# Regrouping the local row loads of a sparse-attention and spectral-mixing kernel, with three edits of its tail

## Chip, cores, metric

One NeuronCore of a Trainium2 chip. The metric is device time in microseconds (us); lower is better. Engines have the profile's names: PE multiplies matrices, ACT is the scalar engine, DVE the vector engine, POOL is GpSimd, SP only issues transfers. "Clock" is the share of PE's full clock that was granted, "PSUM" the memory into which PE writes its results. A trace's span is some 1.8 us shorter than the time of the same run, so spans are compared with spans and times with times.

## The reference, cut to what matters

```python
def _attn_ref(q, k, v):                      # (8, 8, 576, 64), float32
    scores = q @ k.T / sqrt(D)
    # heads 0-3: causal, within 32 rows ("local"); heads 4-7: causal, same position mod 32 ("strided")
    attn = softmax(where(mask, scores, -1e9)); return attn @ v

def _moe_ref(x, w_r, w_i, w_ch):             # x: (8, 576, 512), w: (64, 512, 512)
    X = rfft(x, axis=1)[:, :64]              # 64 modes
    Y = X @ (w_r + 1j * w_i)                 # one 512x512 complex weight per mode
    u = x + irfft(Y, n=576)
    return u + maximum(u @ w_ch, 0)
```

The two weight arrays are 134 MB of float32, 163 MB are read in all. Each of the 64 modes needs weights of its own, 2 MB of float32, and the kernel takes each mode in two halves: 128 half-modes. One request for a pair brings the weights of two half-modes. Where the text and the timelines count modes ("mode 1", "mode 7", "the last mode"), they count half-modes from 0.

## The kernel before

All large loads are issued by GpSimd (POOL) on one queue, in program order, and are converted to fp16 on the way. The attention rows pass through one `ring`: strided rows of batch b take slots 3(b mod 4) to 3(b mod 4)+2, local rows of batch b take slots 2(b mod 6) and 2(b mod 6)+1.

```python
    ring = pat.tile([128, 12, 2048], F16, name="ring")
    ...
    def load_loc(*bs):                       # one batch's local rows per transfer, 288 KB
        for b in bs:
            if b >= B:
                return
            for vi in (2, 0, 1):             # v, q, k
                nc.gpsimd.dma_start(
                    loc_in(b, vi),
                    SRC[vi][b, 0:4].rearrange("h (cb i) d -> (h cb) (i d)", i=18),
                )
```

The strided stage is one iteration per batch. Its last iteration already turns local batch 0 (`loc_front(0)`). `w_fetch(1)` asks for one pair of half-modes (two transfers of 512 KB, from the two weight arrays); one pair is asked for before the loop. Eight pairs fit before any buffer has to be freed; three of the eight (pairs 1, 2 and 7) lie in buffers that are later needed for other things and are not refilled. So the first refill waits for mode 1, the second for mode 7.

```python
    for b in range(B):                       # strided stage
        if b in (1, 3):
            load_str(b + 3, 2)
        load_loc(*[(), (), (), (), (0,), (1, 2), (3,), (4, 5)][b])
        w_fetch([2, 1, 1, 1, 1, 1, 0, 0][b])
        front = str_front(b + 1) if b + 1 < B else loc_front(0)
        ...
    for b in range(B):                       # local stage, with the first 64 half-modes between
        load_loc(b + 6)
        front = loc_front(b + 1)
        ...
            mode(0, sum(NMODES[:b]) + mi)    # after an odd one: w_fetch() into the freed buffer
```

The tail: the last spectra are copied out of PSUM, then 36 units of 128 rows each get two short matmul groups (`v`, `u`), a Relu on ACT, an addition on DVE and a store. `again(n)` repeats a 512-column matmul n times, to keep PE's clock up while it waits for the last weights.

```python
    def spec_out(g, b, tp, zp):
        src, dst = ds(32 * (b % 4), 32), ds(32 * g, 32)
        n = 256 if (g, b) == (3, 0) else 512
        act_copy(zzs[b][dst, 0:n], zp[src, 0:n])              # ACT
        if n < 512:
            nc.vector.tensor_copy(out=zzs[b][dst, n:], in_=zp[src, n:])
        nc.vector.tensor_copy(out=yys[b][dst], in_=tp[src, 0:512])
    ...
            again(0 if m < NM - 6 else 4 if m < NM - 2 else 2)
```

The softmax here doesn't subtract the row's maximum and nothing guards it: scores larger than these inputs give would overflow.

## Time and profile before

| | before |
|---|---|
| time, median of the first 3 runs | 436.13 us (435.8 to 436.99) |
| span of the trace | 433.8 us |
| last weight landed / last mode began | 393.66 / 393.83 us |
| from the start of the last mode to the end | 40.0 us |
| time of the load queue's packets, share of the span | 94.3% |

The landing of the last weight is read from its issue (384.06) and the time to landing of that one transfer (9.6). A line of the profile reads: start and length, engine, source line, operation, written tile <- read tiles; in square brackets how long the engine had been idle before it, and what ended the wait. `wt` is a weight tile, `ring` the attention rows, `y` the modes' accumulators. The chain of waits of the kernel before carries the main reading, that the loads are the bound:

```profile
DMA 69%; PE 18%; DVE 6%; ACT 3%; issue 2%; POOL 1%; DVEq 0%; POOLq 0%
```

### The profile page before, as it was taken

The numbers are of one execution on the slowest core, as the hardware profiler recorded it, in microseconds if no ns is written. First come the engines' busy times: TensorE is split into PE (matmuls) and PEld (weight loads), VectorE is DVE, ScalarE is ACT, GpSimd is POOL, SyncE is SP. The second block draws the span as 40 slices with busy tenths as digits, with TensorE's granted clock in tenths as the row PEclk, the third lists the DMA queues.
The fourth block names the chain that finished last, engine by engine and source line by source line (L and its number), as shares of the span: only waits on it lengthen the run. The fifth ranks groups of instructions, "written<-read, shape, count | busy, mean of one in ns | idle before, by whom it ended". The sixth has DMA issues, their size and how long they took to land.

```text
span 433.8 us, 12099 instructions
## 1 busy us (share of the span) xinstructions
PE 338.7 (78%) x5307; PEld 244.0 (56%) x5307; DVE 215.1 (50%) x466; ACT 188.1 (43%) x353; POOL 128.9 (30%) x208
## 2 busy tenths in 40 slices
PE   1986888779886887889794566698669698977994
PEld 1865776657764665667663344465446465643441
DVE  2888678744523243342511033455346366503895
ACT  1686678635543435445340401133115122602892
POOL 6522332323232222222222222222222221200983
PEclk9999899869967659676855559868798899988999
DMA  8999999999999999999999999999999999991687
GB/s 178 212 213 213 215 212 212 212 210 213 215 212 214 213 214 213 213 214 214 213 213 213 213 213 215 213 213 215 213 213 213 214 213 213 214 179 29 260 331 275
DMA packets 28996, 92.18 MB, mean 212 GB/s; under 512 B 4048, under 2 KB 5072, under 8 KB 28944
## 3 DMA queue, kind: packets, MB, share of 16 engines
q0 software_dynamic: 24704, 81.28, 94.3%
q1 hardware_dynamic: 3440, 9.46, 5.8%
q10 hardware_dynamic: 800, 0.67, 0.6%
q8 instruction: 42, 0.69, 0.6%
q14 instruction: 10, 0.08, 0.0%
HBM read 163.22 MB, written 9.44 MB: 398 GB/s over the span
## 4 chain that ended last, share of the span: by engine, by line
DMA 69%; PE 18%; DVE 6%; ACT 3%; issue 2%; POOL 1%; DVEq 0%; POOLq 0%
DMA wt<-in_moe_w_i_dram 51%; DMA wt<-in_moe_w_r_dram 8%; DMA ring<-in_q_dram 5%; DMA w_ch<-in_moe_w_ch_dram 5%; DVE xb L250 2%; DVE kz L292 2%; PE y L547 2%; PE v L688 2%; PE u L688 2%; PE v L894 2%; PE sc L514 1%; ACT X L260 1%; DVE rec L249 1%; PE tp L395 1%; PE sc L353 1%
## 5 line engine op out<-in xcount | busy, mean ns | idle before, releaser
L547 PE MATMUL y<-X,wt 128*128 128x16 f16 (+1 forms) x2048 | 82.8, 192 | 59.5 <-DMA wt<-in_moe_w_i_dram 58.1
L547 PEld LDWEIGHTS <-wt 128*128 128x128 f16 (+1 forms) x2048 | 73.1, 103 | 75.4 <-issue 68.3
L196 POOL DMA_DIRECT2D wt<-in_moe_w_r_dram x62 | 36.4, 587 | 139.2 <-PE y L547 66.0
L196 POOL DMA_DIRECT2D wt<-in_moe_w_i_dram x60 | 35.2, 587 | 73.0 <-DMA wt<-in_moe_w_i_dram 60.2
L654 ACT ACTIVATE v<-sc 128x512 f16<-128x512 f32 x32 | 19.1, 596 | 68.4 <-PE sc L645 68.3
L471 ACT ACTIVATE PL<-sc 128x480 f16<-128x480 f32 (+1 forms) x48 | 27.7, 579 | 47.6 <-PE sc L457 46.9
L645 PE MATMUL sc<-w_cp,xT 128*128 128x512 f16 (+1 forms) x160 | 47.4, 424 | 0.0
L655 DVE COPY xo<-tp 128x512 f16<-128x512 f16 x32 | 22.1, 692 | 36.7 <-PE tp L653 36.4
L250 DVE TENSOR_TENSOR xb<-av,rec 90x256 f16<-90x256 f32 (+2 forms) x80 | 36.0, 450 | 2.8
L249 DVE RECIPROCAL rec<-av 90x4 f32<-90x4 f32 (+2 forms) x80 | 14.7, 183 | 45.3 <-PE av L486 33.9
L402 DVE COPY qT<-tp 128x576 f16<-128x576 f16 x16 | 12.0, 758 | 40.1 <-PE tp L395 37.2
L260 ACT ACTIVATE v<-tp 128x640 f16<-128x640 f16 (+1 forms) x24 | 19.4, 807 | 24.0 <-PE tp L429 21.1
L395 PE MATMUL tp<-cI_s,ring 64*64 64x64 f16 x864 | 26.4, 211 | 1.6 <-issue 0.8
L360 ACT ACTIVATE PL<-sc 90x360 f16<-90x360 f32 (+1 forms) x48 | 22.7, 490 | 6.2 <-PE sc L353 5.3
L926 DVE TENSOR_TENSOR osb<-u,rl 128x512 f32<-128x512 f32 x36 | 23.6, 689 | 3.3 <-ACT rl L907 1.7
L395 PEld LDWEIGHTS <-ring 64*64 64x64 f16 x864 | 20.7, 123 | 6.8 <-issue 3.6
L441 PE MATMUL sc<-cMl_s,cI_s 128*128 128x480 f16 (+1 forms) x48 | 23.0, 478 | 1.6 <-ACT X L260 1.6
L909 POOL TENSOR_TENSOR rl<-rl,xo 128x512 f32<-128x512 f32 x16 | 18.3, 1155 | 18.9 <-ACT rl L907 18.6
L457 PE MATMUL sc<-qT,kz 128*128 128x160 f16 (+1 forms) x160 | 23.4, 275 | 0.5 <-issue 0.5
L457 PEld LDWEIGHTS <-kz 128*128 128x128 f16 x160 | 16.8, 119 | 10.8 <-issue 8.1
L907 ACT ACTIVATE rl<-v 128x512 f32<-128x512 f32 x36 | 20.4, 597 | 4.9 <-PE v L688 4.2
L285 PE MATMUL tp<-cI_s,ring 72*128 72x72 f16 x256 | 15.1, 206 | 9.5 <-DMA ring<-in_v_dram 8.0
(103 smaller groups left out, 655.5 us busy)
## 6 DMA issues: line engine op xcount, KB each, us to landing
wt<-in_moe_w_r_dram POOLq DMA_DIRECT2D x62, 512.0 KB, 18.9
wt<-in_moe_w_i_dram POOLq DMA_DIRECT2D x60, 512.0 KB, 19.4
out_dram<-osb SPq DMA_DIRECT2D x14, 512.0 KB, 2.7
ring<-in_v_dram POOLq DMA_DIRECT2D x8, 288.0 KB, 13.4
ring<-in_q_dram POOLq DMA_DIRECT2D x8, 288.0 KB, 13.6
ring<-in_k_dram POOLq DMA_DIRECT2D x8, 288.0 KB, 13.0
ring<-in_v_dram POOLq DMA_DIRECT2D x3, 512.0 KB, 15.1
ring<-in_q_dram POOLq DMA_DIRECT2D x3, 512.0 KB, 14.8
```

The costliest lines, as they stand in the source:

```text
L196: nc.gpsimd.dma_start(dst, rows)
L250: nc.vector.tensor_tensor(out=dst, in0=val.rearrange("p h (q c) -> p h c q", c=4), in1=rec[0:n, 0:pieces] .to_broadcast((n, pieces, 64)) . ...
L260: nc.scalar.activation(out=out, in_=in_, func=ACTF.Copy)
L360: nc.scalar.activation(out=PS[0:n, ds(POFF[t], 4 * n)], in_=scp[0:n, 0 : 4 * n], func=ACTF.Exp, scale=SCALE,)
L395: nc.tensor.transpose(tp[ds(64 * hp, 64), ds(64 * i, 64)], qn[ds(64 * hp, 64), ds(64 * (9 * g + i), 64)], idn[ds(64 * hp, 64), ds(64 * hp, ...
L441: nc.tensor.matmul(scp[:, 0 : n * times].rearrange("p (h x) -> p h x", h=times), idn, mask_rows("cMl", n, times), start=True, stop=False,)
L457: nc.tensor.matmul(scp[:, ds(col, n)], kzs[par][:, hp, ds(s0, 128)], qTs[par][:, ds(s0, n)], start=False, stop=(i == len(todo) - 1),)
L471: nc.scalar.activation(out=dst, in_=src, func=ACTF.Exp, scale=SCALE)
L547: nc.tensor.matmul(yv[:, mi, e, :], wt[pr, XC[c], ds(128 * e, 128)], Xh[half][pr, c, :, :, m], start=(c == 0), stop=(c == 3),)
L645: nc.tensor.matmul(vp[pr, :], xT[:, ch, cols], w_chs["cp"][:, ch, :], start=(ch == 0), stop=(ch == 3),)
L655: nc.vector.tensor_copy(out=xo[pr].rearrange("p (h q c) -> p h q c", h=2, c=4), in_=tp[pr, 0:512].rearrange("p (h c q) -> p h q c", h=2, c=4),
L926: nc.vector.tensor_tensor(out=osb[:, t % 2, :], in0=up, in1=rls[b, t][:, t % 2, :], op=AluOp.add)
```

## The change

The intent: fewer, larger transfers (two batches' local rows in one), so that less is paid per transfer; one copy off ACT where ACT holds the tail's start; a finer last store, so that its first half leaves earlier; more repeated passes, so that PE's clock is up when the last weights land.

```diff
-    def load_loc(*bs):
-        for b in bs: ...
+    def load_loc(b):
+        for vi in (2, 0, 1):
+            two = ring[:, ds(2 * (b % 6), 4), :].rearrange("p (b n) x -> p b (n x)", b=2)
+            nc.gpsimd.dma_start(
+                two[:, :, ds(1152 * vi, 1152)],
+                SRC[vi][b : b + 2, 0:4].rearrange(
+                    "b h (cb i) d -> (h cb) b (i d)", i=18
+                ),
+            )
@@ spec_out
-        n = 256 if (g, b) == (3, 0) else 512
-        act_copy(zzs[b][dst, 0:n], zp[src, 0:n])
+        n = {(3, 0): 256, (3, 1): 0}.get((g, b), 512)
+        if n:
+            act_copy(zzs[b][dst, 0:n], zp[src, 0:n])
@@ strided stage
-        load_loc(*[(), (), (), (), (0,), (1, 2), (3,), (4, 5)][b])
-        w_fetch([2, 1, 1, 1, 1, 1, 0, 0][b])
+        w_fetch([2, 1, 1, 1, 2, 0, 0, 0][b])
+        if b > 4:
+            load_loc(2 * (b - 5))
@@ local stage
-        load_loc(b + 6)
+        if b == 1:
+            load_loc(6)
@@ last rows (cut)
+        halves = [ds(0, 256), ds(256, 256)] if i == LAST else [slice(None)]
+        for cols in halves: ...              # addition by halves; then one store per half,
+                                             # the first from ACT, the second from SP
@@ repeated passes
-            again(0 if m < NM - 6 else 4 if m < NM - 2 else 2)
+            again({NM - 1: 2, NM - 2: 3, NM - 3: 10}.get(m, 7 if m > NM - 6 else 0))
```

More of the change, by code (lines that the diff above doesn't have):

```diff
@@ L231, in load_str @@
                 nc.gpsimd.dma_start(two[64:72], src[64:72])
-    def load_loc(*bs):
-        for b in bs:
-            if b >= B:
-                return
-            for vi in (2, 0, 1):
-                nc.gpsimd.dma_start(
-                    loc_in(b, vi),
-                    SRC[vi][b, 0:4].rearrange("h (cb i) d -> (h cb) (i d)", i=18),
-                )
+    def load_loc(b):
[7 more added lines that the diff above has]
+            )
     def v_cols(i):
@@ L925, in u_rows @@
         osb = osbs[b, t]
-        nc.vector.tensor_tensor(
-            out=osb[:, t % 2, :], in0=up, in1=rls[b, t][:, t % 2, :], op=AluOp.add
-        )
+        halves = [ds(0, 256), ds(256, 256)] if i == LAST else [slice(None)]
+        for cols in halves:
+            nc.vector.tensor_tensor(
+                out=osb[:, t % 2, cols],
+                in0=up[:, cols],
+                in1=rls[b, t][:, t % 2, cols],
+                op=AluOp.add,
+            )
         if t == 4:
@@ L934, in u_rows @@
         elif i < 2 or i >= LAST - 1:
-            (nc.scalar if i == LAST else nc.sync).dma_start(
-                out[b, ds(128 * (t - t % 2), 256), :].rearrange(
-                    "(p i) e -> p i e", i=2
-                )[:, t % 2, :],
-                osb[:, t % 2, :],
-            )
+            for j, cols in enumerate(halves):
+                (nc.scalar if i == LAST and j == 0 else nc.sync).dma_start(
+                    out[b, ds(128 * (t - t % 2), 256), cols].rearrange(
+                        "(p i) e -> p i e", i=2
+                    )[:, t % 2, :],
+                    osb[:, t % 2, cols],
+                )
         elif t % 2:
```

## The prediction

> **What bounds the kernel now.** I read the page first (engine shares, slices, transfers), then the chain of waits, then Pool's timeline, then PE's timeline around each stage change.
>
> ```profile
> PEclk9999899869967659676855559868798899988999
> GB/s 178 212 213 213 215 212 212 212 210 213 215 212 214 213 214 213 213 214 214 213 213 213 213 213 215 213 213 215 213 213 213 214 213 213 214 179 29 260 331 275
> L547 PE MATMUL y<-X,wt 128*128 128x16 f16 (+1 forms) x2048 | 82.8, 192 | 59.5 <-DMA wt<-in_moe_w_i_dram 58.1
> ```
>
> The rate is flat at 213 GB/s from the second slice to the 35th: the load queue never runs dry until about 390 us. PE waits 58.1 us in total for weights. The chain of waits agrees: 51% of it is the transfer of the second weight array. So there are two parts: a **load stream** of fixed bytes (last weight used at 393.83 us) and a **tail** of 40 us, which the load stream no longer touches. A change pays only if it shortens the stream, stops it from pausing, or shortens the tail.
>
> Pool's timeline shows how the stream is fed.
>
> ```profile
> 58.64 0.57 POOL L238 DMA_DIRECT2D ring<-in_v_dram  x1 [2.21 <-PE tp L285]
> 59.21 0.56 POOL L238 DMA_DIRECT2D ring<-in_q_dram  x1
> ...
> 70.93 0.54 POOL L238 DMA_DIRECT2D ring<-in_v_dram  x1 [1.15 <-DMA ring<-in_v_dram]
> 72.07 0.54 POOL L238 DMA_DIRECT2D ring<-in_q_dram  x1 [0.60 <-DMA ring<-in_q_dram]
> 73.43 0.54 POOL L238 DMA_DIRECT2D ring<-in_k_dram  x1 [0.82 <-DMA ring<-in_k_dram]
> 75.88 0.60 POOL L196 DMA_DIRECT2D wt<-in_moe_w_r_dram  x1 [1.92 <-DMA wt<-in_moe_w_r_dram]
> ```
>
> The issue at 70.93 is the eighth after the one at 58.64, and it waits for that one to land. So eight transfers are outstanding, and these waits date the landings: batch 0's local v, q, k land at 70.9, 72.1 and 73.4. A 288 KB local transfer takes 1.40 us of stream, a 512 KB weight transfer 2.43. PE needs batch 0's q at 76.65:
>
> ```profile
> 76.65 0.76 PE L395 MATMUL tp<-cI_s,ring 64*64 64x64 f16 x36
> ...
> 79.03 0.47 PE L395 MATMUL tp<-cI_s,ring 64*64 64x64 f16 x18 [0.62 <-DVE qT L402]
> ...
> 95.05 0.62 PE L547 MATMUL y<-X,wt 128*128 128x16 f16 x16
> ...
> 102.99 0.67 PE L547 MATMUL y<-X,wt 128*128 128x16 f16 x16
> ```
>
> No wait for a transfer stands there: batch 0 is about 4 us early. The last two lines are modes 1 and 7, whose ends (95.67, 103.66) free the first two weight buffers for refilling.
>
> The tail, in windows of 3.4 us of PE, then by instruction:
>
> ```profile
> 391.50:394.90 3.40, 2.15 (x37) 0.97 0.14 28
> 394.90:398.30 3.40, 3.40 (x13) 0.53 0.02 5
> ```
>
> ```profile
> 394.85 1.89 PE L886 MATMUL y<-w_ch,YT 128*128 128x512 f16 x4
> ...
> 396.96 1.39 PE L951 MATMUL v<-v,cI_s 128*128 128x512 f16 x3
> ...
> 398.81 1.09 ACT L907 ACTIVATE rl<-v 128x512 f32<-128x512 f32 x2 [1.67 <-PE v L688]
> ...
> 399.93 0.59 ACT L260 ACTIVATE zz<-y 32x512 f16<-32x512 f32 x1
> ```
>
> Busy 2.15 of 3.4 us was followed by a window at clock 0.53 (columns: window, length, busy, clock, DMA share, GB/s). The first tail matmuls run at half rate.
>
> **What the Trainium skill says.**
> - "DMA: Bandwidth & Descriptors", section "Anatomy of one DMA — SWDGE (gpsimd) path": a transfer costs about 2.0 us fixed plus its bytes. Between queued transfers the trace shows none of it: 2.43 us for 512 KB is the stream's rate. It would be paid only when the queue is empty.
> - Same page, "Rules for kernel authors": coalesce small transfers into large ones. In a queue that is never empty, this case gives no sign of a gain.
> - "TensorE: Matmul & The Clock Gate", section on the HAM clock gate: the clock is halved after an idle window of about 3.4 us and restored after a busy one. The trace agrees on the length and the halving (clock 1.00 then 0.53); it shows also that a window 63% busy (2.15/3.4) did not keep the clock.
>
> **The change part by part.**
>
> (1) *Local rows in pairs.* 24 transfers of 288 KB become 12 of 576 KB; bytes and rows are the same. Per row 2304 bytes are still written. All that goes is 12 completions; I allow 0.3 us of stream at most (an estimate: two neighbouring local transfers already follow at 1.40 us, 211 GB/s, against 213 for weights; closing that gap over 33 us of local stream is 0.3 us).
>
> (2) *The new order.* A pair cannot be loaded before the fifth iteration, because it overwrites batch 5's strided v. So the order "batch 0, weights, 1, 2, weights, 3, 4, 5" becomes "weights, weights, 0+1, 2+3, 4+5". The transfer before batch 0's v lands at about 69.2 (Pool's issue of the last k then). Now four weight transfers come first, 4 x 2.43 = 9.7, to 79.0; then v 81.8, q 84.6, k 87.4 at 2.8 each. PE wants q at 76.65 and k at 79.03: it stalls about 8.4 us in the last strided iteration. PE is not the bound there, but it frees buffers. Shifted by 8.4, mode 1 ends at 104.1 and mode 7 at 112.1. The last loads that need no freed buffer (batches 4+5) land at 104.2 by the sum, 105.5 by the trace of the same bytes before. The next weights are issued at 104.2 and, with the skill's 2 us on an empty queue, start at 106.2; their pair takes 4.9, to 111.1; the pair after it waits for mode 7, is issued at 112.3 and starts at 114.3. Pauses: about 1.5 + 3 = 4.5 us. Before, batch 6's rows (4.2 us) filled that hole; now batches 6+7 are issued after the third of these. DVE, cleared during the stall, could win back half a microsecond: I take **+4.0 us**. The stream never makes up a pause, so all of it goes to the end.
>
> (3) *More repeated passes* (20 to 29, at 0.215 us warm). They fill the waits at 390.9 to 392.6 and 393.1 to 393.8, so PE is busy without a gap from mode 59 on. If the clock holds, the four matmuls of 1.89 us take 1.03 (they do so later in the tail), the three passes 0.65 instead of 1.39, mode 63 0.2 less. PE reaches the first spectra matmul 1.5 us earlier (398.40 to 396.9). DVE's second half copy then ends at about 396.5, not in the way. **-1.5 us.**
>
> (4) *Batch 1's copy to DVE.* On ACT 0.59 us goes between the second and third 597 ns activations, and PE waited for the third (0.24 idle, plus slow issue). DVE gains a 32x512 copy of about 0.68 (256 columns took 0.42, 512 of the same kind 0.69) before its first addition at 399.52, where it had 1.14 us idle. **-0.5 us.**
>
> (5) *Last rows in halves.*
>
> ```profile
> 426.91 1.89 DVE L926 TENSOR_TENSOR osb<-u,rl 128x512 f32<-128x512 f32 x3 [0.16 <-PE u L688]
> ...
> 428.23 0.62 SPq L935 DMA_DIRECT2D out_dram<-osb  x1
> 428.83 0.34 ACTq L935 DMA_DIRECT2D out_dram<-osb  x1
> ```
>
> The first half can leave 0.3 us earlier, the second at the same time or 0.1 later, since SP is free at 428.85. The writes queue on shared engines anyway, with 1 KB rows in place of 2 KB. **-0.2 us.**
>
> Sum: -0.3 + 4.0 - 1.5 - 0.5 - 0.2 = +1.5, on 436.1: **437.6 us**.
>
> **The rivals.**
> (A) *The pause is hidden.* If Pool finds buffers sooner, or PE's lag shrinks, the stream never stops: 436.1 - 2.5 = 433.6. For it: PE idles 58 us for weights, so it can catch up; a tuned order was presumably tried. Against: the first refills depend on modes 1 and 7, and PE was busy 7.94 of 8 us between 96 and 104.
> (B) *The pause is longer.* The stall cools PE's clock and the local stage starts at half rate, say 2 to 3 us later: 440.
> (C) *Passes too many.* With a cold clock ten passes last 4.3 us and overrun the wait after mode 61 by about 1 to 2 us; most of the 1.5 gain is lost: 439.
> (D) *Coalescing pays per transfer.* If each removed transfer saved 0.2 us of stream, 12 would save 2.4: 435.5. The flat rate speaks against it.
>
> **Range and chances.** All the terms are under 1.2% together. A and D pull down, B and C up: 433.6 to 441.0. A move of 2% is 8.7 us, which no rival reaches: within 2% 0.96, slower 0.03 (B and C together with a longer pause), faster 0.01.
>
> **What would show it.** Right: PE waits 7 to 9 us for local q near 77; batches 0+1 land at 84 to 88; a slice near 104 to 115 shows a dip of the rate; the last weight lands about 4 us later than 393.7; the window after it has clock 1.00; from the last mode to the end 38 us or less instead of 40. Wrong: no wait for q, no dip, or a half-rate window at the start of the tail. The largest risk is step 2: if the stream does not pause, the result is near 433.6.

## The result

The changed kernel took 440.82 us (median of 4 runs, 439.7 to 442.84) against 435.97 of the kernel before (4 runs, 434.8 to 436.99). Ratios in this document are the mean time of one kernel's fast runs over that of the other's of the same rounds, so they are not quite the ratio of the medians: here **1.0117**, 95% interval 1.0072 to 1.0162. It is slower by about 5 us, within the 2% that counts as "same", inside the stated range, in the stated direction, but three times the +1.5 us that was forecast.

The rate by slices, and the group of matmuls that turn local rows, from the page of the changed kernel:

```profile
GB/s 176 212 214 212 214 213 213 211 213 115 174 212 214 213 214 213 213 215 213 213 212 214 215 213 213 213 214 214 213 214 213 214 213 214 213 213 52 264 326 274
L395 PE MATMUL tp<-cI_s,ring 64*64 64x64 f16 x864 | 25.6, 210 | 8.9 <-DMA ring<-in_q_dram 8.3
```

The flat line of before now has a hole: slices 10 and 11 (98.5 to 120.4 us) ran at 115 and 174 instead of 213. That is (98 + 39) x 10.95 us / 213 = 7.0 us of stream lost. And PE waits 8.3 us for q, where it had no such wait. Pool's timeline of the changed kernel shows the order of events:

```profile
64.39 0.73 POOL L236 DMA_DIRECT2D ring<-in_v_dram  x1 [2.21 <-PE av L374]
65.12 0.72 POOL L236 DMA_DIRECT2D ring<-in_q_dram  x1
66.55 0.72 POOL L236 DMA_DIRECT2D ring<-in_k_dram  x1 [0.71 <-DMA wt<-in_moe_w_r_dram]
...
82.01 0.71 POOL L236 DMA_DIRECT2D ring<-in_k_dram  x1 [2.04 <-DMA ring<-in_v_dram]
105.49 0.60 POOL L196 DMA_DIRECT2D wt<-in_moe_w_r_dram  x1 [22.76 <-PE y L547]
106.08 0.60 POOL L196 DMA_DIRECT2D wt<-in_moe_w_i_dram  x1
112.63 0.59 POOL L196 DMA_DIRECT2D wt<-in_moe_w_r_dram  x1 [5.95 <-PE av L486]
```

After the last rows of the third pair, at 82.01, Pool has nothing that it may load: it is idle for 22.76 us until mode 1 frees the first weight buffer, and again for 5.95 us. That third pair landed 22.6 us after its issue, at 104.6; the next load was asked for at 105.49. PE's timeline of the changed kernel shows why mode 1 was so late:

```profile
84.54 1.17 PE L395 MATMUL tp<-cI_s,ring 64*64 64x64 f16 x36 [8.30 <-DMA ring<-in_q_dram]
...
87.33 1.17 PE L395 MATMUL tp<-cI_s,ring 64*64 64x64 f16 x36 [0.56 <-DMA ring<-in_k_dram]
...
104.53 0.66 PE L547 MATMUL y<-X,wt 128*128 128x16 f16 x16
```

The first line stood at 76.65 before, the last (mode 1) at 95.05: the stall moved mode 1 by 9.5 us. In windows of 2 us of the changed kernel (busy time of PE, weight load, DVE, ACT and Pool, then clock, DMA share and GB/s) the hole is this:

```profile
100.00:102.00 2.00, 1.16 (x14) 0.66 (x15) 0.00 (x0) 0.87 (x4) 0.00 (x0) 0.50 1.06 203
102.00:104.00 2.00, 2.00 (x37) 1.51 (x34) 0.76 (x1) 0.51 (x2) 0.00 (x0) 0.50 0.32 60
104.00:106.00 2.00, 2.00 (x55) 1.77 (x54) 0.37 (x1) 1.12 (x2) 0.51 (x1) 0.83 0.01 1
106.00:108.00 2.00, 2.00 (x67) 1.68 (x65) 1.95 (x5) 0.13 (x1) 0.68 (x2) 1.00 0.69 80
...
112.00:114.00 2.00, 1.99 (x61) 1.87 (x58) 1.43 (x4) 1.30 (x2) 1.18 (x2) 1.00 0.41 70
114.00:116.00 2.00, 1.89 (x33) 1.28 (x31) 0.49 (x1) 0.78 (x2) 1.24 (x3) 1.00 0.98 154
```

Two dips, one around each late request. From 102 on PE is busy throughout, so in this stretch the stream waits for PE, not PE for the stream. The issues of the two late requests, each looked up alone, give their time from issue to landing:

```profile
wt<-in_moe_w_r_dram POOLq DMA_DIRECT2D x1, 512.0 KB, 5.9
wt<-in_moe_w_r_dram POOLq DMA_DIRECT2D x1, 512.0 KB, 5.2
```

The first of them came to an empty queue; the second was issued 1.2 us before the pair ahead of it had landed (112.63 and 113.8). The packets in the trace show how the 5.9 us were spent. The load queue's first packet started at 106.79, 1.3 us after the request; from there to the landing it took 4.6 us, where transfers in the full stream follow one another at 2.43. The data started slowly: in steps of half a microsecond from 106.5 on, the rate was 147, 16, 156 and 156 GB/s before it came to 246. Why is open.

After 116 us the rate is flat again and the loss is carried to the end: the last weight landed at 399.95, 6.3 us later than before (393.66). The tail, from the start of the last mode, took 37.8 us instead of 40.0. The sum, 6.3 - 2.2 = 4.1, is the difference of the two spans (437.9 - 433.8). These are one trace each; the medians of the times differ by 4.9.

### The profile page after: what moved, and what is told of

The parts are those of the page before. It is cut to its first block, busy times and chain, and to the rows that moved or that the text cites. A ratio compares the mean times of both kernels' runs of the same rounds, so it can differ in the third digit from the quotient of the medians.

```text
span 437.9 us, 12103 instructions
## 1 busy us (share of the span) xinstructions
PE 335.8 (77%) x5316; PEld 241.3 (55%) x5316; DVE 215.8 (49%) x468; ACT 187.1 (43%) x352; POOL 124.8 (28%) x196
## 4 chain that ended last, share of the span: by engine, by line
DMA 77%; PE 17%; issue 2%; ACT 1%; DVE 1%; POOL 1%; DVEq 0%; POOLq 0%
DMA wt<-in_moe_w_i_dram 49%; DMA wt<-in_moe_w_r_dram 10%; DMA ring<-in_v_dram 7%; DMA ring<-in_k_dram 5%; DMA w_ch<-in_moe_w_ch_dram 4%; PE y L547 2%; PE v L689 2%; PE v L960 2%; PE u L689 2%; PE v L897 2%; DMA ring<-in_q_dram 2%; PE tp L395 1%; PE sc L514 1%; PE sc L441 1%; PE tp L285 1%
## 5 line engine op out<-in xcount | busy, mean ns | idle before, releaser
L931 DVE TENSOR_TENSOR osb<-u,rl 128x512 f32<-128x512 f32 (+1 forms) x37 | 23.6, 674 | 1.4 <-PE u L689 0.9
L514 PEld LDWEIGHTS <-xb 108*128 108x128 f16 (+2 forms) x176 | 17.2, 115 | 11.4 <-DVE xb L250 5.8
```

The lines of the kernel that those rows point to most:

```text
L514: nc.tensor.matmul(xp[:, ds(192 * cp, 192)].rearrange("p (f m) -> p f m", f=3), xb[b][0:n, base + t, ds(128 * cp, 128)], F[0:n, :, t, :], ...
L931: nc.vector.tensor_tensor(out=osb[:, t % 2, cols], in0=up[:, cols], in1=rls[b, t][:, t % 2, cols], op=AluOp.add,)
```

## The experiments

Twelve kernels ran, all correct. Kernels are compared only within the same rounds. The theory, called P: the load stream pauses because q of batch 0 lands late, so PE frees the first weight buffers late, when nothing else is left to load. Its rivals: M, large transfers are slow in themselves; O, the order alone does it; S, PE's stall reaches the end by itself; T and C concern the tail.

| label | time, us | before | ratio (95%) | last weight landed | last mode to last addition |
|---|---|---|---|---|---|
| changed kernel | 440.82 | 435.97 | 1.0117 (1.0072-1.0162) | 399.95 | 32.8 |
| e5_changed_again | 441.24 | 435.06 | 1.0131 (1.0107-1.0155) | 401.69 | 32.8 |
| e1_order_only | 439.08 | 434.76 | 1.0093 (1.0065-1.0121) | 398.39 | 33.4 |
| e4_wch_in_hole | 439.05 | 434.76 | 1.0094 (1.0065-1.0122) | 398.43 | 33.1 |
| e8_wch_again | 439.56 | 435.06 | 1.0095 (1.0073-1.0116) | 398.49 | 32.8 |
| e3_pairs_first | 434.16 | 434.76 | 0.9972 (0.9941-1.0003) | 394.60 | 33.2 |
| e6_pairs_first_wch | 433.88 | 435.06 | 0.9974 (0.9951-0.9996) | 393.79 | 32.8 |
| e12_both_mends_again | 434.42 | 436.09 | 0.9967 (0.9943-0.9992) | 394.37 | 32.8 |
| e2_tail_only | 433.79 | 434.76 | 0.9969 (0.9942-0.9996) | 394.21 | 32.8 |
| e11_tail_again | 434.91 | 436.09 | 0.9980 (0.9955-1.0004) | 394.48 | 32.8 |
| e7_passes_only | 435.00 | 435.06 | 0.9991 (0.9970-1.0012) | 393.92 | 33.4 |
| e9_copy_only | 435.70 | 436.09 | 0.9997 (0.9969-1.0026) | 393.60 | 34.4 |
| e10_halves_only | 436.24 | 436.09 | 1.0007 (0.9982-1.0033) | 394.18 | 33.5 |

The kernel before has 393.66 and 35.0 in its one trace. Where the stream does not pause, the landing lies between 393.6 and 394.5.

### e1_order_only: the new order, one batch per transfer

```diff
-        load_loc(*[(), (), (), (), (0,), (1, 2), (3,), (4, 5)][b])
-        w_fetch([2, 1, 1, 1, 1, 1, 0, 0][b])
+        w_fetch([2, 1, 1, 1, 2, 0, 0, 0][b])
+        load_loc(*[(), (), (), (), (), (0, 1), (2, 3), (4, 5)][b])
...
-        load_loc(b + 6)
+        if b == 1:
+            load_loc(6, 7)
```

> The kernel before with the new order of loads (two weight pairs, then batches 0, 1, then 2, 3, then 4, 5; 6 and 7 together in the second local batch), but with one batch per transfer and the old tail. Theory P (the stream pauses because the first local rows land late, so the refills of the weight buffers are asked for too late): q of batch 0 lands near 82 instead of 84.5, because batch 1 no longer rides with it, so PE stalls about 5 us, not 8.3; one pause of about 2.8 us remains; last weight near 396.5, total about 438.8. Rival M (the large transfers themselves are slow): no change from before, 436.0. Rival O (the order alone makes the whole loss, however large the transfers are): last weight near 400, 442.2.

PE's wait for q was 3.2 us. The last weight landed 4.4 us later than in the undisturbed runs (about 394.0), and the ratio is 1.0093 with the old tail. Pool's requests, and PE alone in windows of 4 us (busy, clock, DMA share, GB/s), in this run:

```profile
101.29 0.60 POOL L196 DMA_DIRECT2D wt<-in_moe_w_r_dram  x1 [6.96 <-PE y L547]
...
111.15 0.58 POOL L196 DMA_DIRECT2D wt<-in_moe_w_r_dram  x1 [8.67 <-PE y L547]
```

```profile
104.00:108.00 4.00, 4.00 (x83) 0.50 1.07 214
108.00:112.00 4.00, 4.00 (x90) 0.50 0.14 29
```

The first refill came in time; the second came 9.9 us after it (7.1 in the changed kernel), while PE ran at half clock. From the end of mode 1 to the end of mode 7 it took 9.9 us here and 9.9 and 10.0 in two other traces with half clock there (e3, e9), against 7.1 in the changed kernel, at full clock. M falls as the whole cause: without large transfers most of the loss is there. O in its strong form falls too: with pairs the loss of stream is 6.3 and 7.7 us, here 4.4. P was right in kind and too low in size (2.8 expected). What pairing adds is latency: q of batch 0 has to wait for batch 1's v as well. How much of the remaining 2 to 3 us is that, and how much where the clock stood in each trace, one trace cannot say.

### e3_pairs_first: the first pair ahead of the two weight pairs

```diff
-        w_fetch([2, 1, 1, 1, 2, 0, 0, 0][b])
+        w_fetch([2, 1, 1, 1, 0, 0, 0, 0][b])
         if b > 4:
             load_loc(2 * (b - 5))
+        w_fetch([0, 0, 0, 0, 0, 2, 0, 0][b])
```

> The changed kernel with the pair of batches 0 and 1 asked for ahead of the two weight pairs instead of behind them; all else as changed. Theory P: q of batch 0 lands near 75, PE does not stall at 77, the stream carries 104.6 us worth of loads before it needs the first refill, which is asked for by 97; no dip in the rate; last weight near 393.5; total about 433.5. Rival M (pairs are slow in themselves): the last weight stays near 400 and the total near 440.

The wait for local q is gone, and with it nearly all of the loss: 434.16 us, ratio 0.9972, with the same pairs. So the order of the requests is the cause: with the late order and no pairs (e1) most of the loss is there, with pairs and the early order it is not. A small dip is left, to which e6 comes back.

### e4_wch_in_hole and e8_wch_again: other bytes into the hole

```diff
         if b > 4:
             load_loc(2 * (b - 5))
+        if b == 7:
+            w_ch_fetch()
...
-        if b == 6:
-            work.insert(0, w_ch_fetch)
```

> The changed kernel with the one channel weight (512 KB) loaded right behind batches 4 and 5 instead of in the seventh local batch: it needs no freed buffer, so it fills 2.5 us of the hole with bytes that have to be moved anyway. PE's stall of 8.3 us stays. Theory P (the idle stream costs, not PE's stall): last weight 2.5 us earlier than in the changed kernel, total about 438.3. Rival S (PE's stall itself reaches the end): no change, 440.8.

> The changed kernel with the channel weight in the hole, on the same chip as the changed kernel. Theory P: 2.5 us faster than the changed kernel (ratio to it 0.9943) although PE's stall is unchanged at 8 us. Rival S (the stall itself costs): ratio to it 1.0.

PE still waited 7.9 and 5.5 us for q, as the changed kernel did (8.3 and 5.6). Pool's timeline of the first of the two:

```profile
85.61 0.76 POOL L203 DMA_DIRECT2D w_ch<-in_moe_w_ch_dram  x1 [2.06 <-DMA ring<-in_q_dram]
106.28 0.60 POOL L196 DMA_DIRECT2D wt<-in_moe_w_r_dram  x1 [19.91 <-PE y L547]
```

The last weight landed at 398.43 and 398.49 instead of 399.95 and 401.69. On one chip, e8 took 439.56 and the changed kernel 441.24: the ratio of their ratios is 1.0095 / 1.0131 = 0.9964, -1.6 us, where 2.5 was expected; the interval (roughly 0.3% either way, the root of the sum of the two squared) holds the 2.5 too and leaves out zero only just. S, which expected nothing, is unlikely: with the same stall, less idle stream gave an earlier end.

### e6_pairs_first_wch and e12_both_mends_again: both mends

> The changed kernel with both mends: the first pair ahead of the two weight pairs, and the channel weight behind batches 4 and 5. With the pair first alone, a pause of 1 to 1.5 us was left near 107 to 111 (rate slices 201 and 200), because PE's clock was at half there and the second refill was asked for at 107.2. Theory P: 2.5 us more of loads cover it: no dip, last weight 1 us earlier than with the pair first alone, ratio to the kernel before 0.994 to 0.997. Rival M (pairs cost or gain by themselves): ratio outside 0.992 to 0.998.

> Pairs ahead of the weights and the channel weight behind them, with the three changes of the tail, again. If fewer, larger transfers are worth anything in a stream that never pauses, this is faster than the old loads with the same tail; theory P: the two agree within 0.2%.

The rates by slices, from the page of e3_pairs_first and then from that of e6_pairs_first_wch:

```profile
GB/s 174 208 212 214 213 214 212 212 212 201 200 212 213 215 213 214 212 216 211 213 214 213 214 212 214 214 214 214 213 214 214 213 213 215 214 204 41 280 332 257
```

```profile
GB/s 175 209 212 213 213 212 212 213 212 213 213 212 214 213 213 214 214 212 214 214 213 213 213 214 214 214 213 213 213 214 215 213 213 212 214 197 41 268 336 272
```

The dip of 201 and 200 is gone, and the last weight landed 0.8 us earlier, about as much as the landings of undisturbed traces differ among themselves (393.6 to 394.5). The ratio was 0.9974, just above the 0.994 to 0.997 expected, and later 0.9967; both intervals reach into that range. On the third chip e12 and e11, which has the old loads of one batch each and the same tail, gave 434.42 and 434.91, ratios 0.9967 and 0.9980, landings 394.37 and 394.48. Half as many transfers are worth 0.1 us in the trace, less than that spread, and 0.5 us in the medians of six runs, whose ranges overlap (433.76 to 435.05, 434.61 to 435.42). Both versions are a little faster than the kernel before, and that much the tail gives alone (e2 and e11, below); which of them is the better is open.

### e5_changed_again: the changed kernel on another chip

> The changed kernel once more, unedited, so that the next three have it on their chip. Theory P: PE waits 8 us for q of batch 0 again, the rate dips between 102 and 116 us again, about 1.0117 times the kernel before.

The ratio was 1.0131 and the hole was there (slices of 121 and 145). PE's stall was shorter here, 5.6 us, yet the first refill came at 105.77 and the second at 114.46, later than in the first trace; PE's clock was 0.50 from 104 to 108. The stall's length alone does not set the loss: the moment at which modes 1 and 7 end does.

### e2_tail_only and e11_tail_again: the three edits of the tail alone

> The kernel before with only the three changes of the tail (copy on Vector, last rows in halves, more repeated passes), old loads. Theory P: last weight stays at about 393.8, and the tail shrinks from 40.0 to 37.8 us: total about 433.8. Rival T (the tail's gain came only from where the clock's windows fell in that one trace): no change beyond 0.5 us, 435.5 to 436.5.

> The old loads with the three changes of the tail, again, for a comparison on one chip with the next. Ratio 0.9955 to 0.998.

Ratios 0.9969 and 0.9980: about -1.1 us, not -2.2. That e2 met the 433.8 us expected is luck: the kernel before was 1.2 us faster on that chip than on the first. The next three take the edits one by one.

### e7_passes_only: the repeated passes

> The kernel before with only the repeated passes of the last waits changed. Theory C (they hold PE's clock in the first 3 us of the tail, which the old count held in one of two traces): tail of the profile 38.0 to 38.6 us from the start of the last mode against 40.0 and 38.6 in the two traces with the old count; time 0 to 1.6 us less than before, ratio 0.9965 to 1.0. Rival: ten passes overrun the wait and the ratio is over 1.0.

Ratio 0.9991, -0.4 us, not distinguishable from nothing. The reason is in the traces with the old count: of four, two (before, e9) entered the tail at half clock and two (e1, e10) at full clock. PE alone in windows laid onto the clock's own steps, 3.41 us long, the two ahead of and the one into the tail, first e9_copy_only:

```profile
387.88:391.29 3.41, 2.95 (x41) 1.00 0.58 115
391.29:394.70 3.41, 2.01 (x36) 1.00 0.21 42
394.70:398.11 3.41, 3.41 (x12) 0.50 0.02 5
```

and e10_halves_only, with the same passes:

```profile
388.93:392.34 3.41, 2.24 (x24) 1.00 0.53 106
392.34:395.75 3.41, 2.48 (x38) 1.00 0.13 25
395.75:399.16 3.41, 3.37 (x20) 1.00 0.03 7
```

The columns are the window, its length, PE's busy time, clock, DMA share and GB/s. Here a window with 2.01 us of work cost the next one its clock, and windows with 2.24 and 2.48 did not; where the steps fall against the work differs between the two traces. No busy time divides the two outcomes in general: over all full-clock windows of the fourteen traces, laid onto the clock's steps, the clock was lost after up to 2.62 us of work (after 2.48 at 200 us of the kernel before) and kept after as little as 1.58. All ten traces with the new passes had full clock there. But the passes also have a price: in seven of those ten, the last mode began 0.2 to 0.8 us after its weight had landed, against 0.12 to 0.17 in every trace with the old count, because ten passes take 2.15 us and did not fit into the wait. An average saving of half of 1.6 us, less that delay, fits the -0.4; this is an estimate, which no run tests.

### e9_copy_only: batch 1's copy on Vector

> The kernel before with only batch 1's copy moved from Scalar to Vector. Theory: where the clock is full after the last mode, the old tail took 33.4 us from the start of the last mode to the last addition in two traces, and 32.8 with all three changes; the copy alone gives that 0.6 us. Ratio 0.9975 to 0.9995. Rival: the gain is the passes', and this one gives 33.4.

The time shows nothing (0.9997, just outside the 0.9975 to 0.9995 expected, with an interval half a per cent wide that covers it). The trace does: from the last mode to the last addition 34.4 us against 35.0 of the kernel before, both at half clock; at full clock 33.4 with the old copy (e1, e7, e10) and 32.8 with the new (all traces with the three edits but e3 and e4, which have 33.2 and 33.1). So the copy is worth 0.6 us.

### e10_halves_only: the last rows in halves

> The kernel before with only the last rows stored in halves. Theory: from the end of the last addition to the end of the program 4.6 to 5.4 us, as with whole rows (5.0, 5.1, 5.2), because the write queue is full until then; ratio 0.999 to 1.001. Rival: 0.2 us or more earlier in every trace, as predicted.

The ratio is 1.0007. From the last addition to the end of the program it took 5.6 us here; with whole rows 5.0 (before), 5.2 (e1), 5.1 (e7) and 5.5 (e9); with halves in the other traces 4.7 to 5.4. The 5.6 is over the 5.4 expected. No gain shows. In the kernel before, the DMA engines were busy for 0.94 to 0.99 of the time from 427 to 431 us, after the last matmul, which fits the reason expected: the stores already queued set the end.

## Why the prediction was right and wrong

Right: the sign of the whole, the chain of step 2 (rows behind the weights, a stall of PE, two late refills, a pause that nothing makes up), and most of its times. Forecast and measured in the first trace: q at 84.6 and 84.54, k at 87.4 and 87.33, third pair landed at 104.2 to 105.5 and 104.6, second refill asked for at 112.3 and 112.63. The tail of that trace, too, -2.2 and -2.2, but that was luck: the trace of before happened to be in the slower of two outcomes (below). Rival A (hidden pause) fell, and so did D, which needed 2.4 us from merging: e12 is 0.1 us ahead of e11 in the landing and 0.5 in the medians. The 0.3 that step 1 allowed is too small for these runs to test.

**Wrong: the size of the pause, step 2's "+4.0 us".** The first request of the third refill landed at 123.3; without a pause five transfers of 2.43 us after 104.6 would have put it at 116.75. So 6.5 us were lost (6.3 at the last weight). The step that failed is the restart: after a request to an empty queue, step 2 let the data flow at the stream's full rate once 2 us had passed. The difference to 4.0 comes from these terms:

- The restart of an empty queue. Step 2 took "the skill's 2 us" plus 2.43 of data, 4.4 us, and the traces have 5.9 and 5.2 here and 5.1 to 5.8 for the four requests of e1, e5 and e8 that came after all before them had landed. The first packet came 1.3 us after the request, and from it to the landing it took 4.6 us. The first of the two delays was covered by the wait for mode 7; the second cost 0.7 us.
- The second transfer after that second restart took 3.2 us, not 2.43: 0.8 us. After the first restart it took 2.4; why they differ is open.
- "DVE, cleared during the stall, could win back half a microsecond". It did not: mode 1 ended at 105.2, not 104.1, with PE's clock at half from 98 to 104.7. The credit of 0.5 was a guess, and the second refill was 0.3 late besides.
- The start of the hole was averaged (104.2 and 105.5) where 104.6 was right: 0.3 us. The 105.5 was misread, too: in the trace of before these bytes landed at 105.1 (issue 94.20 and 10.9 to landing).

Together they are 2.6, and 6.5 - 4.0 is 2.5; the rest is rounding and a third transfer that was 0.1 quicker.

In the second trace of the changed kernel the clock was worse placed, mode 7 ended at 114.15 (112.33 in the first, 112.1 forecast), and the loss was 7.7 us. So rival B, a start of the local stage "say 2 to 3 us later" at half clock, is in the second trace. In the first, which came to B's 440 as well, it is not: mode 7 was 0.2 us later than forecast, and the slow restarts made the loss.

**Wrong: step 3's "-1.5 us".** The mechanism and the amount hold for a trace that enters the tail at half clock, as the one trace of before did (first Relu 5.0 us after the last mode began, 3.4 with full clock). But I took that trace for the rule, and it was one of two outcomes. Over six runs the passes gave -0.4 us (e7, not distinguishable from nothing), partly, by the estimate above, because of rival C, which came true in a small way (0.2 to 0.8 us of overrun, at full clock). Step 4 held (-0.5 forecast, 0.6 in the traces). Step 5's -0.2 was not there.

The reading of the clock under that step was loose. The prediction says "clock 1.00 then 0.53" where its lines have 0.97 and 0.53, because its windows lay 0.2 us off the clock's steps; on the steps, the trace of before has 1.95 us of work in 3.41 and then 0.50. And its "63% busy did not keep the clock" is no rule (e7).

With the measured terms, 6.3 to 7.7 for the pause and about -1.1 for the tail, the sum is +5.2 to +6.6, and the times gave +4.9 and +6.2 (medians).

## What to carry to other kernels

In this stream of loads, which otherwise never ran empty, the number of transfers mattered little and their order a great deal. So ask of every regrouping which piece is needed first and what now stands ahead of it. Before the point where each further load waits for a freed buffer, count the bytes that can still be loaded against the time until the first buffer comes free, with room for the restart of an empty queue and for a half-rate clock. And do not put a price on an effect of the clock from a single trace: look where its steps fell.

## What the Trainium skill lacked or had wrong

- "DMA: Bandwidth & Descriptors", section "Anatomy of one DMA — SWDGE (gpsimd) path": about 2.0 us fixed plus bytes at 436 GB/s gives 3.2 us for 512 KB (4.4 at this stream's own 2.43 us per transfer). On an empty queue such a transfer, read as 1 MB of float32 and written as fp16, took 5.1 to 5.9 us from issue to landing. The section does not cover a converting load, nor a slow start of the data: 147, 16, 156 and 156 GB/s in the first four half microseconds of the changed kernel's restart, where the stream has 213.
- Same page, "Rules for kernel authors": the advice to coalesce says nothing of a queue that is always full, nor of who waits for the first piece. With the stream full, 12 transfers of 576 KB and 24 of 288 KB ended within 0.1 us of each other (394.37 and 394.48), and behind the weights the larger ones made PE wait 8.3 and 5.6 us for its first piece instead of 3.2.
- "TensorE: Matmul & The Clock Gate", Part 1: idle and busy windows of about 3.4 us are described, but not how busy is busy. Busy time as the profile counts it does not answer it. In the fourteen traces here, full-clock windows of 3.41 us with 1.58 us of work or more could be followed by full clock, and windows with up to 2.62 by half clock. At half clock, no window with less than 2.86 us of work was followed by full clock, but work throughout was not enough either: of 254 such windows, 55 were followed by half clock again (e1 ran without a gap from 104 to 112 us at 0.50).
